# Scores of 26 of 32 head pairs as three float32r products of split queries and keys, on one Trainium2 core

## The chip, the cores and the metric

The kernel runs on one core of a Trainium2 chip. The core has a matrix engine (TensorE, PE in the profile; its weight loads are the row PEld), a vector engine (VectorE, DVE), an activation engine (ScalarE, ACT), a general engine (GpSimd, POOL), and a queue engine (SyncE, SP) that issues all transfers here. The metric is the time of one execution on the device in microseconds; lower is better.

## What is computed

Four batches of 448 positions pass through three stages. The sizes are B = 4, H = 12 heads of 64, S = 448, a model width of 768, and E = 4 experts of head width 64.

```python
# stage one: causal attention per head
scores = where(causal, q @ k.T / 8, -1e9);  a = softmax(scores);  x = a @ v
# stage two: dense, per batch
theta = x @ w_theta
y = w_tok_r @ (x * cos(theta)) + w_tok_i @ (x * sin(theta))
u = x + y;  x = u + relu(u @ w_ch)
# stage three: four experts, each a causal attention, top 2 of 4 by a gate
for e in range(4):
    q, k, v = x @ wq[e], x @ wk[e], x @ wv[e]
    out += gate[e] * (softmax(causal(q @ k.T / 8)) @ v @ wo[e])
```

## The kernel before

The kernel is a program that plans its own order. Every operation is first noted as a step of a `Plan` with an estimated cost (`Plan.cost`), a due time and its dependences; `Plan.rank` carries due times backwards along the dependences, and `Plan.issue` plays a clock over the five engines and hands out the ready step with the earliest due time, engine by engine. What stands in each engine's queue, in which order, and for copies, scalings and subtractions also on which engine (`copy`, `scale`, `combine` name the choices), thus follows from the estimated costs and from the table `K` of numbers (starts, gaps and lengths of the stages). Each engine then works through its queue in order. All instructions are issued from `Plan._emit`, so the profile shows line 478 for nearly all of them, and groups are told apart by tile names.

Heads are handled two at a time by `pair` (L606): 24 pairs of stage one, six a batch (`attn1`), and 8 pairs of experts, two a batch (`attn2`). A pair's input is one tile of 128 rows and 960 columns, head 0 on rows 0 to 63 and head 1 on rows 64 to 127: 512 columns of queries, with zeros laid in so that the last 64 queries of both heads form one block, and 448 of keys. In stage one the tile is `raw`, fetched from memory (three buffers); in stage three it is `qp`, copied out of PSUM after the products with `wq` and `wk` (three buffers).

`pair` computes the scores in three groups, all plain float32:

- `scores([2])`: query block 2 against 384 keys, one product per head into a PSUM bank of its own (tag `sc`, two banks). Each uses half of the array's rows.
- a full-array product of 128 rows and 448 columns for the last 64 queries of both heads together.
- `scores([1, 0])`: blocks 1 (256 keys) and 0 (128 keys), for each head.

After each group DVE adds the mask and takes the row maximum in one custom instruction out of PSUM (shown as CUSTOM_DVE_ANT_0, in the order below as ISA), ACT takes the exponential with its sum, DVE the reciprocal, and POOL or ACT scales. Then TensorE transposes the probabilities (tag `tp`), ACT or DVE copies them to `ph`, and the products with the values (tag `av`) follow.

The dense products are in float32r already: every operand is kept as a high part (rounded to float32r) and a low part (the rest), and `mm3` (L732) adds three products, high by high, high by low, low by high. Weights arrive in a packed or plain form and are split once by `convert` and `widen` on ACT, DVE and POOL during batch 0, then kept in memory (`scr`) as split units. `split` (L600) is the helper that splits a tile: a copy to float32r on ACT, DVE or POOL, and a subtraction on POOL or DVE.

Batches overlap: while TensorE works on the dense products of batch b, the attention of batch b + 1 and the experts of batch b - 1 are laid in between. At the start there is only the attention of batch 0, at the end only the experts of batch 3.

## Time and profile before

| | |
|---|---|
| time, median of 3 runs | 675.13 us (674.04 to 675.37) |
| the profiled execution | 675.52 us; span of its instructions 673.7 us |
| TensorE (PE) busy | 645.6 us, 96%, 3752 products |
| weight loads (PEld) busy | 522.7 us, 78% |
| DVE busy | 418.3 us, 62% |
| ACT busy | 391.0 us, 58% |
| POOL busy | 111.3 us, 17% |
| chain that ended last | PE 83%, DVE 8%, ACT 6% |

The busy time of PE counts from the start of a product to its modelled end, and products overlap, so a busy PE may still be slower than it could be. What a product costs in a stream is read from start to start. A float32 product is recorded as two records, a float32r product as one; both show the type f32. The granted clock is the share of 2.4 GHz that TensorE was given: 1.00 is 2.4 GHz.

### The profile page before, as it was taken

What the parts mean: (1) busy time and instruction counts of PE and PEld (TensorE: products, weight loads), DVE (VectorE), ACT (ScalarE), POOL (GpSimd) and SP (SyncE); (2) the same over time, 40 slices, a digit from 0 to 9 for tenths busy, and PEclk for the clock granted to TensorE, in tenths of its full rate; (3) what the DMA queues carried; (4) which work ended last, traced back from release to release, by engine and by line L of the source; (5) the groups of instructions that cost most, each with busy time, mean ns of one, the idle gap of its engine ahead of it and who ended that gap; (6) DMA issues with size and microseconds to landing.
All of it is one profiled execution on the core that took longest, in us unless ns stands there. A gap on an engine that the chain in (4) does not pass through costs nothing.

```text
span 673.7 us, 11076 instructions
## 1 busy us (share of the span) xinstructions
PE 645.6 (96%) x3752; PEld 522.7 (78%) x3752; DVE 418.3 (62%) x1301; ACT 391.0 (58%) x977; POOL 111.3 (17%) x215
## 2 busy tenths in 40 slices
PE   7997679999999999999999999999999999999997
PEld 5664468778797879877887778788788888997875
DVE  4999999998955586543435677354633457434251
ACT  5999788768724482344557677543555364105374
POOL 3542212222200211000102134100100012001010
PEclk8999979999999999999999999999999999999999
DMA  8845630345788624245536442415541750063243
GB/s 332 282 140 193 241 125 29 110 150 176 273 257 277 220 100 149 88 139 162 166 93 236 154 141 67 139 46 173 148 132 48 229 172 23 24 220 116 64 156 134
DMA packets 46184, 103.13 MB, mean 153 GB/s; under 512 B 4784, under 2 KB 16560, under 8 KB 46128
## 3 DMA queue, kind: packets, MB, share of 16 engines
q1 hardware_dynamic: 46128, 102.43, 46.8%
q8 instruction: 29, 0.48, 0.3%
q14 instruction: 27, 0.22, 0.1%
HBM read 81.15 MB, written 21.26 MB: 152 GB/s over the span
## 4 chain that ended last, share of the span: by engine, by line
PE 83%; DVE 8%; ACT 6%; issue 1%; DMA 1%; POOL 0%; ACTq 0%; POOLq 0%; DVEq 0%
PE mm L478 54%; PE av L478 10%; PE sc L478 9%; PE tp L478 7%; PE cv L478 3%; ACT pa L478 2%; DVE cmb L478 2%; DVE zt L478 1%; ACT zn L478 1%; DVE pa L478 1%; DVE c L478 1%; DVE zn L478 1%; DMA unit<-scr 1%; ACT ph L478 1%; ACT pc L478 1%
## 5 line engine op out<-in xcount | busy, mean ns | idle before, releaser
L478 PE MATMUL mm<-zt,unit 128*128 128x448 f32 x720 | 161.1, 374 | 0.0
L478 ACT ACTIVATE pa<-pa,st 128x384 f32<-128x384 f32 (+2 forms) x262 | 125.3, 492 | 43.1 <-DVE st L478 37.6
L478 PEld LDWEIGHTS mm<-zt,unit 128*128 128x128 f32 x720 | 132.5, 188 | 17.3 <-issue 5.7
L478 PE MATMUL mm<-wt,zn 128*128 128x448 f32 x504 | 124.2, 380 | 0.5 <-ACT zn L478 0.5
L478 PE MATMUL mm<-hl,unit 128*128 128x448 f32 x432 | 103.5, 385 | 6.1 <-DVE zt L478 4.3
L478 PEld LDWEIGHTS mm<-wt,zn 128*128 128x128 f32 x504 | 90.4, 188 | 11.5 <-issue 2.0
L478 PEld LDWEIGHTS mm<-hl,unit 128*128 128x128 f32 x432 | 81.0, 193 | 20.2 <-DVE zt L478 5.5
L478 DVE CUSTOM_DVE_ANT_0 pa<-sc,mask 128x384 f32<-128x384 f32 (+1 forms) x174 | 67.0, 419 | 44.3 <-PE sc L478 37.6
L478 POOL TENSOR_SCALAR pa<-pa,st 128x256 f32<-128x256 f32 (+2 forms) x86 | 46.5, 550 | 256.9 <-DVE st L478 176.8
L478 ACT ACTIVATE ph<-tp 128x512 f32<-128x512 f32 x103 | 56.8, 593 | 44.4 <-PE tp L478 44.1
L478 PE MATMUL sc<-raw 64*128 64x384 f32 (+3 forms) x336 | 69.5, 437 | 2.0 <-DVE st L478 1.7
L478 PE MATMUL tp<-ident,pa 128*128 128x128 f32 x348 | 58.6, 275 | 5.0 <-POOL pa L478 4.1
L478 PEld LDWEIGHTS tp<-ident,pa 128*128 128x128 f32 x348 | 42.9, 141 | 13.0 <-POOL pa L478 5.3
L478 ACT ACTIVATE pc<-pc,st 128x448 f32<-128x448 f32 x56 | 37.4, 667 | 20.0 <-DVE st L478 19.5
L478 PE MATMUL av<-ph,vt 128*64 128x448 f32 (+3 forms) x384 | 46.8, 386 | 2.1 <-ACT xt L478 2.1
L478 PEld LDWEIGHTS av<-ph,vt 128*64 128x64 f32 x384 | 25.4, 136 | 27.4 <-issue 11.2
L478 PEld LDWEIGHTS sc<-raw 64*128 64x128 f32 (+1 forms) x336 | 33.8, 189 | 14.3 <-issue 5.9
L478 DVE TENSOR_TENSOR zn<-cv,zn 128x512 fp32r<-128x512 f32 (+1 forms) x48 | 29.8, 620 | 23.5 <-ACT zn L478 23.4
L478 PE MATMUL mm<-unit,zt 128*128 128x260 f32 (+1 forms) x288 | 40.7, 289 | 0.9 <-DMA unit<-scr 0.9
L478 ACT ACTIVATE zn<-cv 128x512 fp32r<-128x512 f32 (+1 forms) x36 | 19.5, 541 | 34.8 <-PE cv L478 34.7
L478 PEld LDWEIGHTS mm<-unit,zt 128*128 128x128 f32 (+1 forms) x288 | 36.1, 175 | 4.0 <-issue 1.8
L478 POOL MEMSET pc<- 128x64 f32 x32 | 5.0, 161 | 169.5 <-PE tp L478 169.4
(115 smaller groups left out, 893.9 us busy)
## 6 DMA issues: line engine op xcount, KB each, us to landing
unit<-scr SPq DMA_DIRECT2D x96, 384.0 KB, 3.5
scr<-unit SPq DMA_DIRECT2D x32, 384.0 KB, 3.2
raw<-qk SPq DMA_DIRECT2D x24, 480.0 KB, 4.3
c<-w SPq DMA_DIRECT2D x24, 384.0 KB, 3.3
vt<-v SPq DMA_DIRECT2D x24, 256.0 KB, 3.3
unit<-scr SPq DMA_DIRECT2D x18, 260.0 KB, 3.2
c<-scr SPq DMA_DIRECT2D x18, 256.0 KB, 2.8
out<-cmb SPq DMA_DIRECT2D x18, 224.0 KB, 2.7
```

The lines of the kernel that those rows point to most:

```text
L478: getattr(getattr(self.nc, engine), name)(*args, **kw)
```

## The change

For all pairs but the six of batch 0 of stage one, the tile of queries and keys is split into a high and a low part in a new tile `qh` (one buffer, 2 x 960 columns of float32r), and every score product becomes three float32r products that add up in PSUM: high by high, high by low, low by high. In the half-array groups the three terms run outside and the two heads inside, so that products of the two heads alternate. The six pairs of batch 0 keep the float32 products (`halved` is true there). In the planner a float32r product on half of the rows, or with 64-wide weights, now counts as half a cost and as a mode of its own, and the table `K` has other numbers.

```diff
@@ Plan.cost
             if ins[1].dtype != F32:
-                return max(52.0, 8.0 + 0.43 * n)
+                return max(52.0, 10.0 + 0.43 * n) / (2.0 if self.mode(ins, name) else 1.0)
@@ Plan.mode
-        if name != "matmul" or ins[1].dtype != F32:
+        if name != "matmul":
             return 0
         return 1 if ins[0].idx.shape[0] == 1 else 2 if ins[0].width == 64 else 0
@@ the table
-K = {"path": 1.62, ... "ahold": 41360.0, ... "a0": 6370.0, "start": 56960.0, ...
+K = {"path": 1.99, ... "ahold": 40530.0, ... "a0": 7420.0, "start": 57430.0, ...
@@ pair
-        qs = [raw[64 * j:64 * j + 64, :512] for j in range(2)]
-        ks = [raw[64 * j:64 * j + 64, 512:] for j in range(2)]
+        if halved:
+            qk = [raw]
+            terms = ((0, 0),)
+        else:
+            t = sbt([2, 512 + S], F32R, "qh")
+            qk = [t[:, 0], t[:, 1]]
+            split(qk[0], qk[1], raw)
+            terms = ((0, 0), (0, 1), (1, 0))
@@ scores
-                for j in range(2):
-                    pe.matmul(banks[j][:, at:at + n], qs[j][:, 128 * c:128 * c + 128], ks[j][:, :n], start=True, stop=True)
+                for a, b_ in terms:
+                    for j in range(2):
+                        h = slice(64 * j, 64 * j + 64)
+                        pe.matmul(banks[j][:, at:at + n], qk[a][h, 128 * c:128 * c + 128], qk[b_][h, 512:512 + n],
+                                  start=(a, b_) == terms[0], stop=(a, b_) == terms[-1])
@@ the product of the last 64 queries
-        pe.matmul(sc_[:, :S], raw[:, 384:512], raw[:, 512:], start=True, stop=True)
+        for a, b_ in terms:
+            pe.matmul(sc_[:, :S], qk[a][:, 384:512], qk[b_][:, 512:], start=(a, b_) == terms[0], stop=(a, b_) == terms[-1])
```

What stands in the queues now, at three places. First TensorE around a pair of batch 2 that lies among the products with `w_ch` (tag `mm`, from `zt` and `unit`), before:

```order
963 L478 MATMUL sc_3739<-raw_3189 128x384
964 L478 MATMUL sc_3740<-raw_3189 128x384
965 L478 MATMUL mm_3719<-zt_3624,unit_3627 128x448 x2
966 L478 MATMUL mm_3719<-zt_3629,unit_3627 128x448 x3
967 L478 MATMUL sc_3758<-raw_3189 128x448
```

and such a pair now:

```order
1120 L478 MATMUL sc_3782<-qh_3622 128x384
1121 L478 MATMUL sc_3783<-qh_3622 128x384
1122 L478 MATMUL sc_3782<-qh_3622 128x384
1123 L478 MATMUL sc_3783<-qh_3622 128x384
1124 L478 MATMUL sc_3782<-qh_3622 128x384
1125 L478 MATMUL sc_3783<-qh_3622 128x384
1126 L478 MATMUL mm_3730<-zt_3723,unit_3636 128x448
1127 L478 MATMUL mm_3730<-zt_3728,unit_3686 128x448 x3
1128 L478 MATMUL mm_3803<-zt_3700,unit_3691 128x448
1129 L478 MATMUL sc_3805<-qh_3622 128x448 x3
```

Two products have become six, one has become three; dense products still stand between the groups.

Second, DVE at the last group of a stage-one pair (`sc` banks of blocks 1 and 0, the mask, and the sums in `st`), before:

```order
706 L478 ISA pa_3367,st_3368<-sc_3406,mask_67 128x256
707 L478 ISA st_3368 128x1
708 L478 ISA pa_3372,st_3368<-sc_3407,mask_67 128x256
709 L478 ISA st_3368 128x1
710 L478 ISA pa_3367,st_3368<-sc_3406,mask_67 128x128
711 L478 ISA st_3368 128x1
```

and now:

```order
739 L478 ISA pa_3791,st_3792<-sc_3822,mask_67 128x256
740 L478 ISA st_3792 128x1
741 L478 CAST qh_3840<-raw_3266 128x960
742 L478 ISA pa_3798,st_3792<-sc_3823,mask_67 128x256
743 L478 ISA st_3792 128x1
744 L478 TENSOR_TENSOR qh_3840<-raw_3266,qh_3840 128x960
745 L478 ISA pa_3791,st_3792<-sc_3822,mask_67 128x128
746 L478 ISA st_3792 128x1
```

The split of the next pair, a copy and a subtraction of 960 columns, has come between the steps of this pair.

Third, POOL in the front of the program, where batch 0's attention ends (`pa`, `zn` and `pc` hold probabilities, `unit` and `cmb` belong to the conversion of weights), before:

```order
45 L478 TENSOR_TENSOR cmb_496<-c_14_93,cmb_496 128x384
46 L478 TENSOR_SCALAR unit_497<-cmb_496 128x384
47 L478 TENSOR_TENSOR unit_497<-cmb_496,unit_497 128x384
48 L478 TENSOR_SCALAR pa_558<-pa_558,st_597 128x384
49 L478 TENSOR_SCALAR pc_458<-pc_458,st_597 128x448
50 L478 TENSOR_SCALAR zn_550<-zn_550,st_597 128x128
```

and now:

```order
47 L478 TENSOR_TENSOR unit_528<-cmb_527,unit_528 128x384
48 L478 TENSOR_SCALAR zn_558<-zn_558,st_604 128x256
49 L478 TENSOR_SCALAR pa_566<-pa_566,st_604 128x256
50 L478 TENSOR_SCALAR qh_708<-raw_643 128x960
51 L478 MEMSET pc_718 128x64
52 L478 TENSOR_TENSOR qh_708<-raw_643,qh_708 128x960
53 L478 TENSOR_TENSOR cmb_647<-c_99_413,cmb_647 128x384
```

The first split of batch 1 stands on POOL as a whole, between scalings and conversions.

## Rows read from the trace of the kernel before

**Rows 1.** The page: busy time and share of TensorE; the chain by engine.

```profile
PE 645.6 (96%) x3752; PEld 522.7 (78%) x3752; DVE 418.3 (62%) x1301; ACT 391.0 (58%) x977; POOL 111.3 (17%) x215
...
PE 83%; DVE 8%; ACT 6%; issue 1%; DMA 1%; POOL 0%; ACTq 0%; POOLq 0%; DVEq 0%
```

**Rows 2.** Table by stage: length, busy us by engine, granted clock, DMA share, GB/s.

```profile
50.00:100.00 50.00, 36.51 (x196) 25.58 (x193) 49.65 (x145) 41.20 (x102) 10.24 (x17) 0.93 0.57 190
100.00:150.00 50.00, 49.14 (x286) 39.83 (x285) 48.73 (x128) 37.93 (x85) 12.32 (x16) 1.00 0.27 86
150.00:200.00 50.00, 50.00 (x288) 41.77 (x287) 42.10 (x118) 30.48 (x74) 8.22 (x14) 1.00 0.72 238
200.00:300.00 100.00, 99.10 (x579) 83.76 (x578) 60.99 (x183) 48.55 (x118) 12.74 (x25) 1.00 0.48 160
...
600.00:650.00 50.00, 49.73 (x299) 40.61 (x298) 21.63 (x88) 24.03 (x64) 3.78 (x9) 1.00 0.37 114
```

**Rows 3.** Order of time, TensorE around one pair: start, length, operation, shape, records.

```profile
328.86 1.04 PE L478 MATMUL tp<-ident,pa 128*128 128x128 f32 x8
...
331.05 0.92 PE L478 MATMUL sc<-raw 64*128 64x384 f32 x4
331.90 1.29 PE L478 MATMUL mm<-zt,unit 128*128 128x448 f32 x5
333.03 0.91 PE L478 MATMUL sc<-raw 128*128 128x448 f32 x2
333.43 0.93 PE L478 MATMUL mm<-zt,unit 128*128 128x448 f32 x2
334.29 1.95 PE L478 MATMUL av<-ph,vt 128*64 128x448 f32 x16
336.17 0.92 PE L478 MATMUL sc<-raw 64*128 64x256 f32 x8
337.02 5.36 PE L478 MATMUL mm<-zt,unit 128*128 128x448 f32 x25
```

**Rows 4.** Order of time, TensorE: two long runs of float32r products.

```profile
186.23 14.79 PE L478 MATMUL mm<-zt,unit 128*128 128x448 f32 x71
200.87 8.80 PE L478 MATMUL mm<-unit,zt 128*128 128x260 f32 x72
209.59 0.92 PE L478 MATMUL sc<-qp 64*128 64x384 f32 x4
```

**Rows 5.** Groups by line and shape: count, busy us, mean ns, idle before; TensorE.

```profile
L478 PE MATMUL tp<-ident,pa 128*128 128x128 f32 x348 | 58.6, 275 | 5.0 <-POOL pa L478 4.1 <-ACT ph L478 0.9
...
L478 PEld LDWEIGHTS mm<-zt,unit 128*128 128x128 f32 x720 | 132.5, 188 | 17.3 <-issue 5.7
...
L478 PEld LDWEIGHTS sc<-raw 64*128 64x128 f32 x288 | 25.5, 189 | 13.3 <-issue 5.9 <-DVE st L478 4.1 <-DVE cmb L478 0.5
```

**Rows 6.** Groups by line and shape: operations like a split's, and a small one.

```profile
L478 DVE CAST zt<-xt 128x448 fp32r<-128x448 f32 x28 | 11.1, 396 | 3.1 <-PE mm L478 2.6
...
L478 DVE TENSOR_TENSOR zt<-xt,zt 128x448 fp32r<-128x448 f32 x46 | 28.6, 637 | 1.2 <-POOL zt L478 0.6 <-ACT zt L478 0.2
...
L478 ACT ACTIVATE zt<-xt 128x448 fp32r<-128x448 f32 x17 | 9.6, 573 | 29.3 <-PE mm L478 25.5 <-DVE xt L478 3.7
...
L478 POOL TENSOR_TENSOR zt<-xt,zt 128x448 fp32r<-128x448 f32 x2 | 2.3, 1153 | 3.4 <-ACT zt L478 3.4
...
L478 DVE TENSOR_SCALAR st<-st 128x5 f32<-128x5 f32 x32 | 6.5, 203 | 9.2 <-ACT pa L478 9.2
```

**Rows 7.** Order of time: a small DVE operation beside a POOL subtraction.

```profile
54.03 1.15 POOL L478 TENSOR_TENSOR wt<-cmb,wt 128x448 fp32r<-128x448 f32 x1 [2.80 <-DVE wt L478]
...
54.43 0.78 DVE L478 TENSOR_SCALAR st<-st 128x5 f32<-128x5 f32 x1
```

**Rows 8.** Order of time, TensorE: between the last two pairs' scores.

```profile
640.63 2.05 PE L478 MATMUL mm<-unit,zt 128*128 128x260 f32 x15
...
643.42 0.92 PE L478 MATMUL sc<-qp 64*128 64x384 f32 x4
```

## What I predicted, before the result was known

> **What bounds the kernel now.** I read the shares of the page first, then the table by stage, then TensorE's own instructions in order of time around one pair of heads, and last the durations of the operations that a split consists of. TensorE is busy for 96% of the span and the chain of work that ended last runs over it for 83% [rows 1]. The table by stage says where that holds [rows 2]. From 200 us on TensorE is busy 99.10 us of 100, at the full granted clock, and DVE 60.99; from 600 to 650 us it is still 49.73 of 50. From 50 to 100 us it is the other way round: TensorE 36.51 of 50, DVE 49.65. There batch 0's attention, batch 1's first pairs and the conversion of all weights share DVE. From 100 to 150 us both are full (49.14 and 48.73). So a saving on TensorE is worth its full size behind 150 us, about its full size from 100 on, and nothing ahead of 100 us, where a microsecond more on DVE costs a microsecond.
>
> **The change, part by part.**
>
> *Score products.* Of 32 pairs (24 in stage one, 8 in stage two) the six of batch 0 stay, 26 change. In order of time [rows 3], with the pair that starts at 331.05 us: the group for query block 2 (384 columns, two heads) holds TensorE from its start to the start of the next product for 331.90 - 331.05 = 0.85 us; the group for blocks 1 and 0 (256 and 128 columns, two heads) for 337.02 - 336.17 = 0.85; the full-array product of 448 columns with the two float32r products behind it for 334.29 - 333.03 = 1.26, which leaves 1.26 - 2 x 0.206 - about 0.1 for the turn to the next shape = 0.75. At 2.4 GHz (the granted clock is 1.00 there [rows 2]) 448 columns take 0.187 us and 384 take 0.160. Four passes make 0.747 and 0.640, so a float32 product is four passes, the two heads already run at the same time, and a group of half-array products pays some 0.21 for the turn.
>
> A float32r product of 448 columns takes (200.87 - 186.23) / 71 = 0.206 us and one of 260 columns (209.59 - 200.87) / 72 = 0.121 [rows 4]: one pass (0.187, 0.108) and 0.013 to 0.019 more. For 128 columns there is no float32r row. The nearest is the transpose of 128 columns: eight end 1.04 us after the first starts [rows 3], one alone lasts 0.275 [rows 5], so (1.04 - 0.275) / 7 = 0.11 each, twice the pass of 0.053. I take 0.110 for 128 columns, since a row of this length sets it, and 0.053 as the lower bound. Whether two float32r heads run at once no row shows; that two float32 heads do is the nearest row, so I take yes.
>
> The new cost of a pair: 448 columns 3 x 0.206 = 0.62 instead of 0.75, so -0.13. 384 columns 3 x 0.178 = 0.53 instead of 0.64, -0.11. Blocks 1 and 0: 3 x (0.107 + 0.013) + 3 x 0.110 = 0.69 instead of 0.64, +0.05: here the three products are no gain, as the short ones don't reach their pace. The sum is **-0.19 us a pair**. Lower bound, with bare passes: -0.19 - 0.16 - 0.16 = -0.51. Upper bound: the rival on reloads, below. 23 pairs lie where TensorE is the bound (26 less the three of batch 1 that start at or ahead of 90 us): 23 x -0.19 = **-4.4 us**.
>
> *The splits.* Each of the 26 pairs gets a copy to float32r and a subtraction over 960 columns. By the order of instructions, of the copies 16 stand on DVE, 9 on ACT, 1 on POOL, of the subtractions 22 on DVE and 4 on POOL. Scaled by columns from 448 (an upper bound, as each has a fixed part) [rows 6]: copy on DVE 0.396 x 960/448 = 0.85, on ACT 0.573 x 2.14 = 1.23, subtraction on DVE 0.637 x 2.14 = 1.37, on POOL 1.153 x 2.14 = 2.5. That is at most 16 x 0.85 + 22 x 1.37 = 44 us on DVE, 11 on ACT, some 11 on POOL. Behind 200 us DVE idles 39 of 100 us, and the 20 pairs there bring it some 20 x 2.2 = 44 us over 474: TensorE's other products cover them. If that cover were gone, a pair's first scores would come 0.85 + 1.37 and two hand-overs later, some 2.5 us.
>
> *The front, up to some 200 us.* Here DVE counts. The splits of batch 1 give DVE three subtractions and one copy, at most 5.0 us; ACT gets four copies, POOL one copy and three subtractions. By the order of instructions eleven products and subtractions of the weights' conversions (tiles unit, cmb and c) leave DVE for POOL, and six of their copies come to DVE. At 0.6 and 0.4 us a piece, from the rows of like width [rows 6], that is -6.6 + 2.4. So DVE's load in the front stays within 1 us of what it was, and POOL's grows by some 11 x 1.1 + 9 = 21 us. POOL has the time, but it and DVE get in each other's way: a DVE operation on 5 columns, 0.20 us in the mean, took 0.78 beside a POOL subtraction [rows 6, 7]. I take +1.0 us, nearest to the unchanged sum of DVE; the bounds are -1 and +6.
>
> *The single split buffer* (tile qh): a pair's split can't begin before the scores of the pair ahead are done. The tightest place is the end: from the end of the last pair but one's scores to the last pair's first group 643.42 - 640.63 = 2.8 us pass [rows 8], the split needs 2.2 and hand-overs. It fits, and new work (the columns of the last values tile) stands between them. I cost it at nothing; if it didn't fit, 0.5 us.
>
> *Planner numbers and the mode of 64-wide float32r products* only move the order. Of that I take no gain and no loss behind 150 us.
>
> Sum: 675.5 (the profiled execution's own time; span 673.7) - 4.4 + 1.0 = 672.1. The median of the runs shown lies 0.4 below the profiled one: **671.7 us**, own range 668.5 to 674.5. About 0.2% (1.35 us) is what a measurement of this kernel can tell from no change.
>
> **The rivals.**
>
> *The front gives it back (slower).* Place: DVE from 50 to 150 us, full [rows 2]. POOL's 21 us more, of which up to a quarter to a third lands on DVE operations that wait as the one of 0.78 us does, and ACT's copies, which delay batch 1's first pairs. Price +6 instead of +1: 675.5 - 4.4 + 6 - 0.4 = 676.7. It decides against the change from 4.4 us on. For it: DVE at 49.65 of 50 and the row of 0.78 us. Against it: DVE's own sum is unchanged, and POOL is busy only 10.24 and 12.32 of 50 us there [rows 2].
>
> *Nothing to see.* In-order TensorE waits at the score groups for the splits: 0.15 us a pair, 23 times, is 3.4. 675.1. For it: the split stands between the softmax steps of the pair ahead on DVE. Against it: TensorE is idle less than 1 us of 100 behind 200 us [rows 2] with the same kind of hand-over today.
>
> *Reloads wait in their own rows (slower).* If the next weights of a head could be loaded only when its product ahead is through, the groups would pay 2 and 5 more loads of 0.109: -0.16 - 0.16 + 7 x 0.109 - 0.13 = +0.31 a pair, 23 x 0.31 + 1 - 0.4 on 675.5 makes 683. Against it: the group of blocks 1 and 0 loads twice as often as that of block 2 for the same columns (8 records against 4) and takes the same 0.85 us [rows 3]. The Trainium skill, "TensorE: Matmul & The Clock Gate", Part 3 (Packing small matmuls), "What overlaps and what doesn't", states just this rule: a weight load overlaps a product in flight only in another row group. For float32 the rows contradict it; for float32r no row decides.
>
> *Not side by side.* If the float32r products of the two heads ran one after the other, a pair would take 0.53 + 0.69 more: +1.03 a pair, 675.5 + 23.7 + 1 - 0.4 = 700. Nothing in the trace speaks for it; float32r on half the rows just doesn't occur there.
>
> *The passes alone count.* With no overhead and short products at 0.053, -0.51 a pair: 675.5 - 11.7 + 1.0 - 0.4 = 664.4. For it: the float32 groups show no such overhead. Against it: the 0.013 to 0.019 of [rows 4] and the transposes. The same page of the Trainium skill, "Weight-path perf modes — Fast Weight Load (FWL) and DoubleRow", says that 128 weights of a type other than FP32 load faster; then the short products alone would come to 0.066 and the total to about 668.7. The trace disagrees so far: a load of float32r weights lasts 188 ns, of float32 weights 189 [rows 5].
>
> **How the numbers follow.** Forecast 0.46, passes alone (or part of it) 0.12, nothing to see 0.12, front 0.18, reloads 0.07, not side by side 0.05. Faster by over 0.2% (under 673.8): 0.40 of the forecast, 0.12, and 0.03 of nothing to see: 0.55. Within 0.2%: 0.06 + 0.09 + 0.02 of the front = 0.17. Slower: 0.16 + 0.07 + 0.05 = 0.28. The range runs from the passes alone, 664, to the front's upper part, 679; reloads, one after the other and a tail of the front stay out.
>
> **What would show it.** In the trace after: two score records of the two heads a few ns apart, groups of 384 columns at about 0.75 us from start to next start, those of 256 and 128 at about 0.9, the 448 products at 0.206 each. DVE busy some 35 us more in all, and TensorE's busy share behind 200 us still 99%. Wrong in its first step if the groups of 256 and 128 fall well under 0.85 (short products cheaper) or a group exceeds 1.2 (reloads, or one after the other); wrong in its front if the first token product (mm from wt and zn) starts over 2 us later than in the trace before.

## The result, and the profile after

| | before | after |
|---|---|---|
| time, median | 674.79 us (673.54 to 675.37) | 679.56 us (678.52 to 682.0) |
| ratio after to before | | 1.0079, 95% interval 1.0059 to 1.0099 |
| span of the profiled execution | 673.7 us | 677.5 us |
| first token product (`mm` from `wt` and `zn`) starts | 106.35 us | 115.00 us |
| first values product (`mm` from `unit` and `zt`, 260 columns) starts | 200.87 us | 208.58 us |

The change makes the kernel 0.8% slower. I had forecast 671.7 us with a range up to 679. The two start times divide the span: up to the first values product the kernel after is 7.7 us late, from there to its end it is 3.9 us quicker (468.9 instead of 472.8 us). So the loss lies in the front (all that comes ahead of the first values product), and the gain behind it is there but smaller.

The page of the kernel after, busy time by engine and the chain that ended last; they answer to [rows 1]:

```profile
PE 642.6 (95%) x3934; PEld 535.7 (79%) x3934; DVE 455.9 (67%) x1330; ACT 399.1 (59%) x984; POOL 135.5 (20%) x231
...
PE 70%; DVE 14%; ACT 1%; issue 1%; DVEq 0%
```

DVE has 37.6 us more work, about the 35 that I expected, and its share of the chain grew from 8% to 14%. The table by stage of the kernel after (columns as in [rows 2]) says where:

```profile
50.00:100.00 50.00, 38.54 (x241) 28.78 (x241) 48.54 (x140) 44.60 (x107) 19.63 (x22) 0.93 0.51 169
100.00:150.00 50.00, 41.76 (x231) 34.36 (x232) 46.83 (x107) 32.44 (x72) 18.65 (x21) 0.86 0.20 67
150.00:200.00 50.00, 49.52 (x302) 41.88 (x302) 47.98 (x130) 32.41 (x78) 13.83 (x19) 1.00 0.69 230
200.00:300.00 100.00, 98.07 (x583) 86.77 (x582) 65.35 (x177) 45.58 (x104) 15.45 (x26) 1.00 0.53 172
300.00:400.00 100.00, 99.89 (x661) 83.85 (x660) 59.67 (x199) 62.17 (x161) 14.47 (x34) 1.00 0.51 163
400.00:500.00 100.00, 99.83 (x615) 84.50 (x614) 63.29 (x172) 54.65 (x136) 14.44 (x28) 1.00 0.38 122
```

Behind 300 us TensorE is busy 99.8 us of 100, so what the splits add there hardly stops it. From 100 to 150 us it is busy 41.76 us where it was 49.14, at a granted clock of 0.86 where it was 1.00, and DVE, the engine that is the bound in the front, is busy 48.54 + 46.83 = 95.37 us of the 100 from 50 to 150 where it was 98.38 [rows 2].

A stretch of fixed length does not show how much work stood ahead of a milestone. Up to the first values product, in the same columns, the kernel before and then the kernel after:

```profile
0.00:200.87 200.87, 181.46 (x1033) 137.48 (x1034) 179.17 (x537) 151.49 (x382) 52.88 (x99) 0.97 0.57 192
0.00:208.58 208.58, 182.18 (x1075) 141.39 (x1075) 187.95 (x536) 152.97 (x383) 74.90 (x115) 0.95 0.55 184
```

DVE is busy 8.8 us longer up to this point and idle 20.6 us instead of 21.7; POOL is busy 22.0 us longer. In this kernel, then, DVE's work ahead of the milestone has grown, and not its idle time.

TensorE around one pair of batch 2, kernel after, in order of time; it answers to [rows 3]:

```profile
326.14 0.79 PE L478 MATMUL sc<-qh 64*128 64x384 f32 x6
326.85 1.29 PE L478 MATMUL mm<-zt,unit 128*128 128x448 f32 x5
327.98 0.77 PE L478 MATMUL sc<-qh 128*128 128x448 f32 x3
328.59 1.39 PE L478 MATMUL mm<-zt,unit 128*128 128x448 f32 x6
329.92 0.91 PE L478 MATMUL sc<-qh 64*128 64x256 f32 x12
330.75 2.52 PE L478 MATMUL mm<-zt,unit 128*128 128x448 f32 x11
```

In this pair, from start to next start, the group of 384 columns holds TensorE for 0.71 us (it was 0.85), the 448 columns for 0.61 (0.75), blocks 1 and 0 for 0.83 (0.85): 0.30 us saved a pair.

The front, TensorE in order of time, first of the kernel before, up to its first token product:

```profile
103.34 0.60 PE L478 MATMUL cv<-ident,zt 128*128 128x128 f32 x4
...
105.99 0.49 PE L478 MATMUL cv<-ident,zt 128*128 128x128 f32 x3
...
106.35 3.67 PE L478 MATMUL mm<-wt,zn 128*128 128x448 f32 x17
```

and of the kernel after (in brackets the idle time ahead of the group, and who ended it):

```profile
93.47 3.81 PE L478 MATMUL mm<-hl,unit 128*128 128x448 f32 x18
97.20 0.92 PE L478 MATMUL sc<-qh 64*128 64x256 f32 x12
104.63 1.11 PE L478 MATMUL cv<-ident,zt 128*128 128x128 f32 x4 [6.51 <-DVE zt L478]
107.16 0.90 PE L478 MATMUL cv<-ident,zt 128*128 128x128 f32 x3 [1.42 <-DVE zn L478]
108.75 6.41 PE L478 MATMUL mm<-hl,unit 128*128 128x448 f32 x18 [0.69 <-DVE zt L478]
115.00 3.85 PE L478 MATMUL mm<-wt,zn 128*128 128x448 f32 x18
```

TensorE, which works in order, stands for 6.51 us at a transpose of `zt` which DVE has not made yet; behind it the same 18 products that took 3.81 us at 93 us take 6.41. DVE and its neighbours at that moment, kernel after, in order of time:

```profile
98.08 2.61 POOL L478 TENSOR_TENSOR zt<-zt,xt 128x448 f32<-128x448 f32 x2 [5.39 <-ACT zt L478]
98.09 1.61 DVE L478 SCALAR_TENSOR_TENSOR cmb<-zt,cmb 128x448 uint32<-128x448 uint32 x1
...
98.97 0.99 ACT L478 ACTIVATE qh<-raw 128x960 fp32r<-128x960 f32 x1
99.63 4.11 DVE L478 TENSOR_TENSOR zt<-zt,xt 128x448 f32<-128x448 f32 x2
...
100.66 2.59 POOL L478 TENSOR_TENSOR qh<-raw,qh 128x960 fp32r<-128x960 f32 x1
```

This looks like my rival of the front to the letter: a subtraction of batch 1's split on POOL, and beside it two DVE operations that take 4.11 us (one such operation took 0.679 us in the mean of the kernel before). The experiments were made to see whether it is the cause.

### The profile page after: what moved, and what is told of

Its sections match the earlier page's. It is cut to its first block, busy times and chain, and to the rows that moved or that the text cites. A ratio compares the mean times of both kernels' runs of the same rounds, so it can differ in the third digit from the quotient of the medians.

```text
span 677.5 us, 11509 instructions
## 1 busy us (share of the span) xinstructions
PE 642.6 (95%) x3934; PEld 535.7 (79%) x3934; DVE 455.9 (67%) x1330; ACT 399.1 (59%) x984; POOL 135.5 (20%) x231
## 4 chain that ended last, share of the span: by engine, by line
PE 70%; DVE 14%; ACT 1%; issue 1%; DVEq 0%
PE mm L478 48%; PE av L478 8%; PE sc L478 6%; PE tp L478 5%; DVE zt L478 3%; DVE cmb L478 3%; PE cv L478 2%; DVE zn L478 1%; DVE c L478 1%; DVE pa L478 1%; DVE qh L478 1%; DVE unit L478 1%; DVE st L478 1%; DVE xt L478 1%; DVE hl L478 0%
## 5 line engine op out<-in xcount | busy, mean ns | idle before, releaser
L478 ACT ACTIVATE pa<-pa,st 128x384 f32<-128x384 f32 (+2 forms) x263 | 126.9, 495 | 40.2 <-DVE st L478 35.0
L478 PE MATMUL sc<-qh 64*128 64x128 f32 (+3 forms) x546 | 69.6, 323 | 5.8 <-DVE st L478 3.7
L478 PEld LDWEIGHTS sc<-qh 64*128 64x128 f32 (+1 forms) x546 | 46.8, 186 | 20.5 <-DVE st L478 8.2
L478 ACT ACTIVATE pc<-pc,st 128x448 f32<-128x448 f32 x53 | 35.3, 666 | 15.9 <-DVE st L478 15.5
L478 ACT ACTIVATE zn<-cv 128x384 fp32r<-128x384 f32 (+1 forms) x34 | 18.2, 534 | 37.7 <-PE cv L478 34.8
L478 PE MATMUL cv<-ident,zt 128*128 128x128 f32 x168 | 28.3, 281 | 7.9 <-DVE zt L478 6.5
```

What stands on the lines that cost most here:

```text
L478: getattr(getattr(self.nc, engine), name)(*args, **kw)
```

## The experiments

All times are medians, and each ratio is to runs of the kernel before on the same chip. The last three columns are read from TensorE's order of time: start of the first token product, of the first values product, and the end of the span (106.35, 200.87 and 673.7 in the kernel before).

| run | time, us | ratio, 95% interval | token | values | end |
|---|---|---|---|---|---|
| after | 679.56 | 1.0079 (1.0059 to 1.0099) | 115.00 | 208.58 | 677.5 |
| e1_split_on_dve | 678.28 | 1.0040 (1.0025 to 1.0054) | 114.49 | 208.08 | 676.5 |
| e2_no_subtractions | 675.03 | 0.9994 (0.9983 to 1.0006) | 113.20 | 206.76 | 674.7 |
| e7_warm | 684.89 | 1.0138 (1.0122 to 1.0155) | 120.17 | 213.45 | 682.5 |
| e9_f32_products | 686.83 | 1.0170 (1.0143 to 1.0197) | 116.42 | 210.92 | 686.3 |
| e3_numbers_alone | 689.87 | 1.0216 (1.0199 to 1.0234) | 116.42 | 210.05 | 687.8 |
| e4_old_numbers | 692.79 | 1.0257 (1.0238 to 1.0277) | 122.42 | 220.67 | 690.5 |
| e5_batch1_f32 | 680.66 | 1.0079 (1.0061 to 1.0098) | 116.24 | 209.81 | 680.1 |
| e6_batch1_f32_old_numbers | 680.15 | 1.0068 (1.0043 to 1.0093) | 110.11 | 205.75 | 679.2 |
| e13_planner_costs | 685.67 | 1.0154 (1.0124 to 1.0184) | 109.86 | 205.58 | 683.5 |
| e12_one_number | 683.75 | 1.0124 (1.0088 to 1.0159) | 109.81 | 207.91 | 682.1 |
| e10_order_kept | 703.94 | 1.0428 (1.0398 to 1.0458) | 111.08 | 210.90 | 702.1 |
| e11_order_kept_late | 692.06 | 1.0248 (1.0213 to 1.0282) | 106.12 | 200.66 | 691.4 |
| e15_front_kept_old_table | 678.81 | 1.0057 (1.0035 to 1.0079) | 105.28 | 199.81 | 675.9 |
| e17_front_kept_back_planned | 673.43 | 0.9983 (0.9970 to 0.9995) | 106.65 | 201.19 | 671.6 |
| e18_front_kept_other_table | 672.57 | 0.9963 (0.9949 to 0.9978) | 105.03 | 201.01 | 670.0 |
| e19_table_alone | 676.32 | 1.0014 (1.0003 to 1.0025) | 105.85 | 201.78 | 674.1 |
| e20_front_kept_f32_products | 678.56 | 1.0042 (1.0027 to 1.0057) | 106.25 | 202.22 | 675.8 |
| e21_front_kept_no_subtractions | 672.63 | 0.9963 (0.9951 to 0.9975) | 106.04 | 201.99 | 672.0 |

### The suspects at the 6.5 us: POOL, the subtractions, the clock

In the first three runs the order of instructions is that of the kernel after; the edit is made in `_emit`, where instructions are handed out. The split instructions of POOL go to DVE:

```diff
@@ _emit
         for engine, name, args, kw in step.calls:
+            if engine == "gpsimd" and args and isinstance(args[0], View) and args[0].root.tag == "qh":
+                engine = "vector"
```

> The changed kernel with every instruction in the same order; the five instructions of splits that stood on POOL (one copy, four subtractions) are issued on DVE at the same place. Port theory (a POOL subtraction over 960 columns holds DVE up, and TensorE's wait then costs clock): the front regains 4 us of DVE's wait and some 2.5 us of slow clock, less 4 to 5 us of new DVE work partly in its place: 674 to 676, token products start 3 to 6 us earlier than in the changed kernel. Load theory (DVE and ACT simply have more to do): 680 to 683. Order theory (the planner's new numbers lay the front out worse, splits or not): 679 to 680.

The subtractions are left out altogether, and the high parts stand in the products in place of the low ones:

```diff
+            if name == "tensor_tensor" and args[0].root.tag == "qh":
+                continue
+            if name == "matmul":
+                args = [self.high(a) for a in args]      # the high part in place of the low one
```

> The changed kernel in the same order without the 26 subtractions of the splits; the low part is left out of the computation, and each score is three times the product of the high parts, so TensorE's work stays as it is. Port theory and load theory: the front is as early as in the kernel before or earlier, 670 to 674. Order theory: still 677 to 680.

And 56 transposes that nobody reads stand ahead of the transposes that wait:

```diff
+            if name == "transpose" and args[0].root.tag == "cv" and not hasattr(self, "warmed"):
+                self.warmed = True
+                for _ in range(56):
+                    self.nc.tensor.transpose(args[0].ap(), args[2].ap(), args[2].ap())
```

> The changed kernel with 56 transposes that nobody reads, some 6 us, laid ahead of the transposes at which TensorE waits 6.5 us for DVE at 98 us. If the half clock after that wait costs 2.5 us: 677. If DVE sets the pace there whatever the clock: 679 to 680.

POOL's splits on DVE brought the first values product 0.5 us forward, no subtractions at all 1.8 us, of 7.7. The first figure is a balance: three subtractions and a copy, 4.1 us, came to DVE ahead of that product, and DVE's busy time up to it stayed what it was (187.77 us), so the freedom from POOL and the moved work cancelled. The second run has neither, and 5.9 us of the loss are still there:

```profile
0.00:206.76 206.76, 184.11 (x1075) 143.12 (x1075) 181.27 (x532) 152.70 (x383) 67.88 (x112) 0.93 0.56 186
```

DVE's busy time is within 2.1 us of before, and its idle time has grown to 25.5 us in place of 21.7. So neither the subtractions beside DVE on POOL nor their load on DVE is the main part of the front's loss. In the whole they are worth more: the ratio is 0.9994 in place of 1.0079, some 5.7 us. The profiled execution, the longest of its ten, shows 2.8 of them (677.5 to 674.7): 1.8 in the front and 1.0 behind it. Where the others lie is not shown. The third run did not do what it was made for. TensorE, kernel with the extra transposes, in order of time:

```profile
97.64 0.91 PE L482 MATMUL sc<-qh 64*128 64x256 f32 x12
105.01 7.91 PE L476 MATMUL cv<-ident 128*128 128x128 f32 x56 [6.46 <-DVE zt L482]
...
116.36 3.97 PE L482 MATMUL mm<-hl,unit 128*128 128x448 f32 x18 [1.05 <-DVE zt L482]
```

The 56 transposes waited with the step that they were put into, and ran behind the wait. It tells two other things. The 18 products now took 3.97 us instead of 6.41, with other work between the wait and them, so 2.4 us of the front's loss lie in TensorE's pace after a long wait; the granted clocks stand in the last section. And the 4.9 us by which the first values product came later than in the kernel after (213.45 against 208.58) stand in the end (682.5 against 677.5): in this order a microsecond lost in the front is lost for good.

### The products by themselves

Same order, splits kept, one float32 product from the plain copy in place of the three:

```diff
+            if name != "identity" and isinstance(args[0], View) if args else False:
+                if args[0].root.tag == "qh" and name != "tensor_tensor":
+                    args = (args[0].f32(),) + args[1:]
+                if name == "matmul" and args[1].root.tag == "qh":
+                    if not kw["start"]:
+                        continue
+                    args, kw = (args[0], args[1].f32(), args[2].f32()), {"start": True, "stop": True}
```

> The changed kernel in the same order with its splits, but every score product is one float32 product of the same tile (copied, not rounded) instead of three float32r ones. What the products themselves are worth: 20 to 23 pairs at 0.28 us (the groups measured 0.92, 1.03 and 0.61 in a stream against 1.04, 1.05 and 0.75) make 5.6 to 6.4 us more: 685 to 686. If TensorE's saving is worth nothing: 679 to 680.

With float32 products the kernel has a ratio of 1.0170 instead of 1.0079: the three products are worth 0.0091 of 675, some 6 us, 0.24 us for each of the 26 pairs. What I predicted of the products holds, and it is more than I took. If the pieces add up, this gives an estimate of what the 0.0079 of the kernel after is made of: the products -0.0091, the subtractions +0.0085, and what is left, order and copies together, +0.0085. Each is good to some 2 us.

### A new order of the front, with and without splits

All pairs float32 and no split at all, with the table and the planner's costs of the change:

```diff
-            xhl[b, pr] = pair(fetch, [vt[:, j] for j in range(2)], None, xp, due, gap, b == 0, tag)
+            xhl[b, pr] = pair(fetch, [vt[:, j] for j in range(2)], None, xp, due, gap, True, tag)
...
-            hl.append(pair(lambda: qps[r], [v2[r][:, :, j] for j in range(2)], g7[:, r, :], None, due, gap, False))
+            hl.append(pair(lambda: qps[r], [v2[r][:, :, j] for j in range(2)], g7[:, r, :], None, due, gap, True))
```

> All 32 pairs in float32 without splits, but with the new table of numbers and the new planner costs. Order theory (the numbers lay the front out worse, with or without splits): token products start 4 us or more later than in the kernel before, 679 to 683. Load theory (the splits' work in the front is what costs): 674 to 677, token products start within 2 us of before.

The change with the old table `K`:

> The changed kernel with the table of numbers of the kernel before (planner costs as changed). Order theory: the front is within 2 us of before and the products keep their 5 to 7 us: 668 to 672. Load theory: the front stays 5 us or more late: 674 to 680.

The change with batch 1 float32 too (`b <= 1` in place of `b == 0`), so that the front holds no split, with the new table and then with the old one:

> The changed kernel with its new numbers, but batch 1's six pairs of stage one stay in float32 as well, so that no split lies ahead of 200 us. Order theory: the front is still 4 us or more late, 677 to 681. Load theory: the front is as before and 20 pairs keep 0.28 us each: 669 to 671.

> As the run before, but with the old table of numbers. Both theories: front as before, 20 pairs at 0.28 us gained, 668 to 671; if the stretches behind 200 us have waits of their own from the splits, 671 to 675.

Without a split in the front the first values product starts at 210.05 and 209.81 with the new table, later than the 208.58 of the kernel after. The loss is there with no split. All pairs float32 (e3_numbers_alone), up to the first values product:

```profile
0.00:210.05 210.05, 185.38 (x1033) 139.15 (x1033) 180.88 (x535) 150.26 (x380) 57.05 (x103) 0.95 0.54 183
```

DVE is busy 1.7 us longer than before and idle 29.2 us instead of 21.7, and POOL has only 4.2 us more. What is left is the order. Two runs below test it alone.

The old table did not bring the old front back, as I had expected for e4_old_numbers (668 to 672) and e6_batch1_f32_old_numbers (668 to 671): the planner's changed costs alone make another order. It also shows that splits in the front are not free. With the old table the first values product is 4.9 us late without batch 1's splits and 19.8 us late with them, so there the splits, and the order that the planner makes for them, cost 14.9 us; with the new table the two stand 1.2 us apart, the other way round.

Two runs take the kernel before, with its work unchanged, and only make the planner lay it out anew. One has the two lines of the planner's costs:

```diff
-                return max(52.0, 8.0 + 0.43 * n)
+                return max(52.0, 10.0 + 0.43 * n) / (2.0 if self.mode(ins, name) else 1.0)
...
-        if name != "matmul" or ins[1].dtype != F32:
+        if name != "matmul":
```

> The kernel before with two lines changed and nothing else: the planner's cost of a float32r product and its mode for float32r products on half the rows. No score product is split, the table of numbers is the old one; the planner only lays out the same work in another order (from the 65th instruction of ACT on, the 108th of TensorE). Order theory: the front loses 3 to 15 us with the same work, first values product at 204 to 216, 678 to 690. Rival (the order costs nothing, the losses of the changed kernel come with the new work): 674 to 677.

The other has one number of the table changed by 2%:

```diff
-K = {"path": 1.62, ...
+K = {"path": 1.65, ...
```

> The kernel before with one number of its table changed by 2% (path, 1.62 to 1.65), nothing else; the same work in another order. If the order of before is tuned to the microsecond and any other is worse by some us: 677 to 690, lost ahead of 200 us. If the order is forgiving: 674 to 677.

They lose 1.5% and 1.2% in the whole, and 4.7 and 7.0 us of that ahead of the first values product, with not one split and no float32r score product in them. The table by stage of the kernel with one number changed:

```profile
50.00:100.00 50.00, 38.99 (x212) 28.39 (x210) 46.65 (x136) 40.27 (x97) 8.99 (x16) 0.89 0.59 187
100.00:150.00 50.00, 46.15 (x256) 37.04 (x252) 43.80 (x112) 33.48 (x74) 15.84 (x22) 0.93 0.25 79
```

DVE is busy 90.45 us of these 100; in the kernel before 98.38. In the front DVE is the bound, and the order of the kernel before leaves it 1.6 us of idle time there. This new order leaves 9.6, that of the kernel after 4.6. Of the orders of the front that this study saw, only that of the kernel before loses nothing, and a change that moves the planner's costs, or numbers of the table that reach the front, gives it up.

### The old order, with the splits put in between

In these two the planner works with the old costs and table on float32 products, and `_emit` puts the copy and the subtraction of a pair on DVE as soon as its queries and keys are there and the scores of the pair ahead are done by the planner's clock:

```diff
@@ Plan.splits, called after each step that is handed out
+            p["qh"] = t = self.pool_sb.tile([P, 2, 512 + S], F32R, tag="qh0", name=f"qh_{self.serial}", bufs=1)
+            raw = p["raw"].real
+            self.nc.vector.tensor_copy(t[:, 0], raw)
+            self.nc.vector.tensor_tensor(t[:, 1], raw, t[:, 0].bitcast(F32), op=OP.subtract)
```

All other instructions stand on every engine in the order of before. First with batches 0 and 1 float32:

> The order of the kernel before, instruction for instruction on every engine, with its table of numbers; only the score products of the 24 pairs from batch 2 of stage one on are three float32r products, and the copy and the subtraction of such a pair stand on DVE in between, from the moment the pair's queries and keys are there. Batches 0 and 1 keep their float32 products, so that the full front holds no split. Twenty of the 24 pairs or more lie behind 150 us. Order theory (the change loses in the front because its instructions stand in another order there, and its products save 0.28 us a pair): first token product within 0.5 us of the 106.35 of the kernel before, first values product within 1 us of 200.87, end 20 to 22 x 0.28 = 5.6 to 6.2 us earlier: 668 to 671. Load theory (splits anywhere cost what the products save): 674 to 677.

then with batch 1 split as in the change:

> As the kernel with the order kept and two batches left float32, but batch 1 also has split products, so the work is that of the change, in the order of the kernel before, with every split on DVE. In the full front DVE gets the splits of batch 1: 4 x (0.65 + 1.15) = 7.2 us of which those of three pairs lie ahead of 100 us. Order theory: the front loses at most these 5 to 7 us and more likely half of them, as the products of batch 1 become shorter: first values product at 201 to 207, 669 to 675. Load theory: as after in the front, first values product at 208 or later, 678 to 682.

My forecast of 668 to 671 for the first was wrong by more than 20 us. Its front is as before to 0.2 us, so the order does carry the front. But 17.9 us go behind it. One place of that kernel, in order of time:

```profile
418.81 0.65 DVE L480 CAST qh<-raw 128x960 fp32r<-128x960 f32 x1
...
419.49 1.16 DVE L481 TENSOR_TENSOR qh<-raw,qh 128x960 fp32r<-128x960 f32 x1
...
423.86 0.61 DVE L522 TENSOR_TENSOR hl<-av,hl 128x448 fp32r<-128x448 f32 x1
...
424.53 1.08 PE L522 MATMUL av<-hl,c 128*128 128x448 f32 x4 [1.65 <-DVE hl L522]
...
428.94 0.62 DVE L522 COPY cmb<-av 128x448 f32<-128x448 f32 x1 [3.20 <-PE av L522]
```

The split of 1.8 us stands ahead of a row of DVE steps that ends in the subtraction for `hl`, and TensorE waits 1.65 us for that one. Soon after DVE is idle for 3.20 us. The free time is there, but in a queue that works in order it only covers what stands in it. The table by stage of this kernel:

```profile
200.00:300.00 100.00, 96.59 (x596) 83.60 (x596) 65.39 (x182) 47.04 (x110) 13.80 (x25) 1.00 0.48 156
300.00:400.00 100.00, 94.00 (x604) 78.13 (x603) 55.19 (x181) 56.14 (x152) 12.90 (x28) 1.00 0.53 162
400.00:500.00 100.00, 95.11 (x586) 79.51 (x585) 63.36 (x172) 53.80 (x133) 17.35 (x31) 1.00 0.36 109
```

TensorE idles 3 to 6 us of each 100 where the planned kernel after idles 0.1 to 1.9, with DVE at 55 to 65 us in both. The second run adds what splits cost in the full front. The copies and subtractions of all six pairs of batch 1 stand on DVE ahead of the first values product, 12.5 us in all, and it comes 10.2 us later than without them (210.90 against 200.66). Ahead of the first token product stand three of them, 6.2 us, and it comes 5.0 us later. So where work is laid on DVE in the full front in the old order, it costs about four fifths of its size, with what batch 1's shorter products give back already in it.

### The front left alone, the splits planned behind it

These keep batches 0 and 1 float32 and give the planner the old costs for all products that were there before, so that the front comes out in the old order; the split pairs behind it are planned. The old table:

```diff
-            xhl[b, pr] = pair(..., b == 0, tag)
+            xhl[b, pr] = pair(..., b < 2, tag)
@@ Plan.cost
+                if ins[1].root.tag == "qh":      # and the same test in Plan.mode
+                    return max(90.0, 10.0 + 0.43 * n) / (2.0 if self.mode(ins, name) else 1.0)
+                return max(52.0, 8.0 + 0.43 * n)
```

> The same program with the old table, so that all work stands as before up to some 190 us and the splits behind are planned with due times that were set for a kernel without them; the planner's own end is then only 0.3 us earlier than for the kernel before. Theory (the splits need their own due times): the front as before, 673 to 677. If due times behind the front don't matter: 667 to 671.

and two tables that differ from it only in numbers for work behind the front (`len` 108840 to 109162 and 106523, `av1` 2.73 to 2.68 and 2.6, and some more), taken from a search over such numbers for an early end by the planner's own clock:

> Batches 0 and 1 of stage one float32, all later pairs as three float32r products with copy and subtraction; the planner's costs of the products that were there before unchanged and its table of numbers changed only where it sets due times of work behind the front (chosen so that the planner's own end is early). By the order of instructions all engines' rows up to the channel products of batch 0 (at about 148 us) stand as in the kernel before. Theory (the front's order was lost by planning it anew, and the products save 0.28 us a pair where the planner has laid the splits into DVE's free time): first token product and first values product within 1 us of before (106.35, 200.87), TensorE busy over 99% behind 200 us, 20 pairs or more x 0.28 = 5.6 us or more earlier: 667 to 671. Rival (a split costs DVE and so TensorE behind the front what its products save, as where the order was kept and splits put in between): 674 or more.

> The same program with another table for the work behind the front, found by the same search from another start; its planned end is 0.2 us later. Tells whether the result hangs on one lucky order. Theory: 667 to 672. Rival: 674 or more.

Both are faster than the kernel before, by 0.17% and 0.37%, though not by as much as I had expected (667 to 671 and 667 to 672 us); the second, at 672.57 us, is the fastest of this study. The table by stage of it:

```profile
50.00:100.00 50.00, 36.44 (x189) 25.88 (x190) 49.67 (x140) 41.54 (x100) 9.73 (x15) 0.93 0.54 182
100.00:150.00 50.00, 49.14 (x286) 39.73 (x285) 48.61 (x127) 37.08 (x85) 12.06 (x15) 1.00 0.27 96
200.00:300.00 100.00, 98.69 (x607) 85.75 (x606) 66.82 (x192) 52.78 (x125) 11.89 (x23) 1.00 0.49 163
300.00:400.00 100.00, 99.67 (x657) 83.60 (x656) 59.64 (x198) 62.21 (x160) 12.89 (x31) 1.00 0.53 166
400.00:500.00 100.00, 99.84 (x618) 85.18 (x617) 57.77 (x164) 57.99 (x145) 14.60 (x26) 1.00 0.38 117
```

DVE is busy 98.28 us of 100 in the front, as in the kernel before, and TensorE 99.67 and 99.84 of 100 from 300 to 500 us, about as in the kernel after: each part as in the better of the two. But the gain of 2.5 us is not the 5.6 to 6 of 20 pairs. The old table with the same program is slower than before (1.0057), so what comes behind the front depends on its order as well.

### What the gain of 2.5 us is made of

The same order as in the fastest kernel, with float32 products (the edit of e9_f32_products), then without subtractions (that of e2_no_subtractions), and last the kernel before with its table:

> The kernel with the front kept and the other table, every instruction in the same order, its copies and subtractions kept too; only the score products of the split pairs are float32 again, one product from the plain copy in place of three. Tells what the three products alone are worth in this order. If they save 0.28 us a pair where TensorE is the bound: 20 to 22 pairs, 5.6 to 6.2 us more than the 672.57 with split products: 678 to 680. If they are worth more or less here than in the order of the changed kernel (7.3 us for 26 pairs), the difference stands in the end.

> The same order again with the three products, but without the 20 to 24 subtractions; the high part stands three times in the products, so the low parts are left out of the scores. Tells what the subtractions still cost behind the front. If TensorE's other products cover them fully: 672 to 673. If they explain what is missing between 5.6 us and the 2.1 us gained: 669 to 671.

> The kernel before with nothing but the other table of the kernel with the front kept: no split, all products float32, the front in the old order. Tells whether that table alone is the gain. If the gain is the products': 674.5 or more, as the planner's own end is 0.2 us later than with the old table. If the table is the gain: 671 to 673.5.

In ratios to the kernel before: the table alone 1.0014; with the copies and subtractions of the splits, products float32, 1.0042; with the three products 0.9963; without the subtractions 0.9963. So the table is not the gain, it costs 1 us; the splits cost 0.0028, some 1.9 us; the products give 0.0079, some 5.3 us; and the subtractions are covered. The 1.9 us are then the copies or the way in which steps come to stand; no run tells these apart. The intervals are 0.0011 to 0.0015 to either side, so each of these pieces, a difference of two ratios, is good to some 1.3 us.

## Why the prediction was wrong

**Score products: right mechanism, under-sized.** I had -0.19 us a pair; the rows show -0.30 (0.14 at 384 columns, 0.14 at 448, 0.02 at blocks 1 and 0). The short ones were the unknown: I took 0.110 us for 128 columns, from the transposes. Of the 0.83 us of blocks 1 and 0, 0.21 for the turn and 3 x 0.120 for 256 columns leave 0.087 for 128. The two heads run side by side; one after the other the six products of 384 columns would take 6 x 0.178, not 0.71. The rival on reloads fell too: it charged blocks 1 and 0 three more loads of 0.109 us than block 2, 0.33 us for the same columns, and the difference is 0.12. That no row decided this for float32r was a misreading of mine: a float32r product of 448 columns started every 0.206 us [rows 4], each with a load of 188 ns [rows 5], so the loads ran beside the products. The rule of the Trainium skill ("TensorE: Matmul & The Clock Gate", Part 3, "What overlaps and what doesn't") that a weight load overlaps a product in flight only in another row group does not bind for float32r here either.

**Cover behind 200 us: right in one planned order, open in that of the change.** TensorE stayed at 98.07 to 99.89 us of 100, and in e21_front_kept_no_subtractions taking the subtractions away gained nothing. But I gave as the reason that DVE idles 39 of 100 us. That reason is not enough: in e11_order_kept_late DVE idles as much, and TensorE lost 17.9 us. And the gain behind the front was 3.9 us, where 20 pairs of 0.30 would be 6.0. Of the difference, the profiled execution of e2_no_subtractions shows 1.0 (208.58 to 677.5 is 468.9 us, 206.76 to 674.7 is 467.9), and by the medians the subtractions may have cost more there. What else is missing is not shown; the new order of the back is the likely rest, and no run measured it by itself.

**The single split buffer** cost next to nothing: the list of waits of the kernel after has TensorE's scores waiting once for `qh`:

```profile
PE sc L478 <- DVE qh L478: 1.2, 1, 1.2
```

**The front: the step that failed.** The test that I had named for it, a first token product over 2 us later, came out at 8.65 us. I put "+1.0 us, nearest to the unchanged sum of DVE", with 6 as the upper bound; it was 7.7. Two terms of this were wrong.

The first is the sum itself. I had DVE's load in the front within 1 us of what it was; up to the first values product it was 8.8 us more (187.95 against 179.17). This alone is not the loss: without subtractions it was 2.1 us more, and 5.9 us of the loss stayed.

The second, and the larger, is the order. The order of before kept DVE busy for 98.38 us of 100, and I read that as a property of the stage and not of the order. I wrote that planner numbers "only move the order. Of that I take no gain and no loss behind 150 us", and gave the order in the front no price of its own. The runs show that price: 4.7 and 7.0 us with the work of before laid out anew (e13_planner_costs, e12_one_number), 9.2 with the table and costs of the change and no split (e3_numbers_alone); and between -1.1 and +1.4 in the seven runs that kept the front's order and had no split in it. That last spread says how far single traces of nearly the same front stand apart, so the 0.5 us of e1_split_on_dve is not clear of it.

My rival of the front had the place and nearly the price (+6), and POOL's 22.0 us more are the 21 that it names. But its mechanism, POOL and DVE in each other's way, did not carry the price: without any subtraction of a split on either engine 1.8 us of the 7.7 came back. The conversions that had moved to POOL stayed there in that run; in e3_numbers_alone POOL has 4.2 us more than before, and the loss is larger than in either.

**What stays open.** How the 5.9 us that stay without the subtractions divide between the order and the copies of batch 1's splits: no run has the order of the change without the copies. Batch 1's splits cost 10.2 us when they are laid into the old order on DVE, and no run shows whether there is an order that carries them without loss. Nor is it shown where 2.9 of the 5.7 us lie that leaving out the subtractions saves by the medians.

## What to carry to other kernels

When a change makes a scheduler lay out a program anew, price the new order as a term of its own: run the kernel before with one scheduling number moved by 2%, and see what that alone costs. Idle time of an in-order engine hides new work only if that work is put where the idle time is. And when a gain shows in one stage and a loss in another, pin the order of the losing stage and let only the other one change.

## What was not expected of the hardware

Two DVE operations on two tensors of 448 columns took 4.11 us beside POOL subtractions, and one on `cmb` 1.61 us, shown in the front above; in the mean of the kernel before one of the two took 0.679, and the one on `cmb` 0.617. In e2_no_subtractions, where POOL starts a little later, the one on `cmb` took 0.63, while the two still took 3.03:

```profile
98.80 0.63 DVE L488 SCALAR_TENSOR_TENSOR cmb<-zt,cmb 128x448 uint32<-128x448 uint32 x1
...
99.05 2.84 POOL L488 TENSOR_TENSOR zt<-zt,xt 128x448 f32<-128x448 f32 x2 [6.52 <-ACT zt L488]
99.35 3.03 DVE L488 TENSOR_TENSOR zt<-zt,xt 128x448 f32<-128x448 f32 x2
```

So the two engines held each other up far more than the quarter to a third that I had taken, for as long as both ran operations on two tensors. The Trainium skill, "SBUF — State Buffer", "SBUF: two separate sides", states a reason: of a DVE operation with two inputs in SBUF and a POOL operation that reads SBUF, the one that starts first holds a shared pair of ports for its whole instruction, and the other waits. The trace agrees in that 4.11 us is three times what the two operations take elsewhere. It still was not what cost most of the front.

TensorE's clock was the other surprise. The wait of 6.51 us ends at 104.63 us. Behind it the granted clock of the kernel after is 0.50, the lower of its two levels (1.2 GHz), and over the 18 products from 108.75 us on it is 0.56; in e7_warm, with the extra transposes between, the same 18 ran at 1.00 (the third line):

```profile
104.63:108.75 4.12, 2.01 (x7) 1.22 (x7) 4.12 (x9) 2.74 (x7) 0.00 (x0) 0.50 0.00 0
108.75:115.00 6.25, 6.25 (x18) 5.57 (x19) 5.85 (x20) 3.77 (x12) 1.16 (x1) 0.56 0.00 0
116.36:120.17 3.81, 3.81 (x19) 3.49 (x20) 3.81 (x15) 2.17 (x7) 1.17 (x1) 1.00 0.02 4
```

So the wait cost 2.4 us on top, in the products behind it (6.41 against 3.97 us).
